# Pooled q and k of the first batch on GpSimd, and longer transfers in the plan, in a kernel whose order a planner writes

## The chip, the cores and the metric

The kernel runs on one core of one Trainium2 chip. The metric is the device time of one execution in microseconds (us); less is better. Three runs of the kernel before took 880.1, 879.05 and 879.85 us (median 879.85). The profile is of a further execution that took 879.63 us, of which 877.9 us are the span of its instructions.

## The reference

Attention comes first, then two dense layers. The inputs q, k and v are (4 batches, 8 heads, 576 positions, 64) in float32.

```
q_d, k_d, v_d = means of q, k, v over groups of 4 neighbouring positions   (144 positions)
out_up    = softmax(q_d k_d^T / 8) v_d, each row repeated 4 times
out_local = softmax over |i - j| < 4 of (q k^T / 8), times v
x = (out_up + out_local) as (2304 tokens, 512)
y   = (h * sigmoid(h), with h = x @ w_in) @ w_out                 # 512 -> 2048 -> 512
out = (h2 if h2 > 0 else exp(h2) - 1, h2 = y @ w_in2) @ w_out2    # the same sizes
```

## The kernel before

One stream of work is cut into jobs, and a planner inside the kernel's Python code decides, while the program is built, in which order each engine gets them. On the chip every engine then works its own list strictly in that order: an instruction at the head of a list that has to wait holds up all behind it.

**Jobs.** `Job(eng, dur, fn, preds, ...)` has an engine (P TensorE, V VectorE, A ScalarE, G GpSimd, S the transfer queue of SyncE), a reckoned duration, what it needs, buffers that it takes and gives back, and a due time. `alike(...)` makes a job that may run on either of two engines; the planner takes the one that would end earlier, with a bias from `PREFER`. `pick()` takes the job that can start first; between those that could start within 0.05 us it takes the one with the earlier due time, and on TensorE a job of the same kind as the last one is favoured by `STICK`. Transfers have a reckoned length: `D_ROWS` for q and k, `D_LOCAL` for windows of v, `D_V` for v to be pooled, `D_W` for a weight tile. `clock_of` says when each engine is first free in the plan.

**Fillers.** Up to the first full unit of the first dense layer, whenever the plan sees TensorE idle for longer than 0.1 us, `fill()` puts matmuls on zeros there (L370), one for each 0.22 us of the gap.

**Attention.** `attend(i, due)` makes the jobs for one pair of heads of one batch (16 pairs, 4 a batch). Rows of q and k are loaded, transposed on TensorE (L653), copied out of PSUM (L681, L686). `pool_qk` (L695) sums q and k over 4 neighbours, one VectorE reduction each. Local scores (L773, for batch 0 with the mask put in by matmul, L765) go through maximum, subtraction, exponential, sum, normalization (L784 on GpSimd) and transposition (L900). Pooled scores (L847) go through maximum (L861), exponential (L869), normalization (L886 on GpSimd), transposition (L921). L939 and L1005 multiply with v, L1022 joins both into x. `hED` is the tile of the pooled exponentials; batch 0 has two, `ring2` and a part of `yo`.

**Weights.** Tiles of 512 KB of the first dense layer land in three staging tiles (`ws`; one more is lent). `decode_jobs` turns the words of a tile into floats: two ScalarE passes (L426, L430) and three VectorE passes (L434, L437, L441); then ScalarE and GpSimd split each into a high and a low part (L1101, L1105). The next load into a staging tile waits for L441. Tiles are counted from 0; even ones are of w_in, odd ones of w_out.

**Dense layer 1** runs beside attention on blocks of 256 tokens: a unit is one product with a w_in tile (L1124, 12 matmuls, in chunks of 3 for the first two blocks), tanh on ScalarE, L1153 on VectorE, a split in two parts (L1155 on ScalarE, L1158 on GpSimd) and a product with a w_out tile (L1172, 12 matmuls). At most two PSUM banks hold units between L1124 and L1153. From some 200 us on, TensorE runs the remaining dense work (L1500, L1588, L1590) back to back.

Of the kernel before, what the change touches and what calls it, by code (L numbers as in the profile page):

```python
# [15 lines left out]
ALU = mybir.AluOpType  # L16
# [6 lines left out]
def attention_moe_moe2_kernel(ctx, tc, q, k, v, wi1, wo1, wi2, wo2, out):  # L23
# [29 lines left out]
    WIN = 64  # L53
    WARM = 9
    PREFER = {("G", "V"): 1.0, ("V", "G"): -1.0, ("A", "V"): 0.5, ("V", "A"): -0.5}
    PACKED, PE_POOLED, HALVED, CHUNKED, STICK, T_SECOND = 0, 1, 0, 4, 3, 40.0
    STICK_FROM = 0
    BACKLOG = 3.0
    D_ROWS, D_LOCAL, D_V, D_W, S_ROWS, S_LOCAL, X_AFTER = 1.6, 1.9, 1.5, 2.2, 1.1, 2.2, 1
    QUAD_FROM, MASK_PE = 0, 1  # L60
    FILL_TO, SAFE_R, SAFE_W = (0, 0), 0.0, 0.0
    LEND = 1
# [86 lines left out]
    cand, blocked = [], set()  # L149
    events = {}  # L150
    now = [0.0]
    clock_of = {"A": 0.0, "V": 4.0, "G": 4.0, "S": 0.0, "P": 5.0, "dma": 0.0, "port": 4.0}
    filling = [True]
    serial = [0]
    mode_of = [None]
# [252 lines left out]
    def decode_jobs(i, out, preds, takes=(), temp=None):  # L408
# [8 lines left out]
        if i < 2 * FP:  # L417
            held = [Hold(WS)]
            wst[i] = held[0]
            landed[i] = Job("S", 0.55, lambda: load_w(i), [], takes=held, dma=D_W, safe=SAFE_W)  # L420
        else:
            landed[i] = Job("S", 0.55, lambda: load_w(i), [decoded[i - WS_N]] if i >= 2 * FP + WS_N else [decoded[n] for n in range(2 * FP)], dma=D_W, safe=SAFE_W)

        def first():
            st = pairs_of(wst[i])
# [153 lines left out]
    def attend(i, due):  # L579
# [57 lines left out]
        def row_of(which, j, c):  # L637
            return (hq, hk)[which].tile[:, (j * NTB + c) * D:(j * NTB + c + 1) * D]

        copies = []  # L640
        prior = []
        for n_, cells in enumerate(([(0, c) for c in range(NTB - 1)], [(1, c) for c in range(NTB - 1)], [(0, NTB - 1), (1, NTB - 1)])):
            bank = Hold(banks, "a")
# [20 lines left out]
            for which in range(2):  # L664
                n = TB * sum(w == which for w, _ in cells)
                if n:
# [24 lines left out]


        def pool_qk():
            for which, src in enumerate(hqk.tile):
                nc.vector.reduce_sum(hqkD.tile[:, which * SD:(which + 1) * SD], src.rearrange("p (m r) -> p m r", r=FAC), axis=AX.X)  # L695

        red = Job("V", 1.48, pool_qk, copies, takes=[hqkD], uses=[hqk])
        vd = lambda: hvd.tile.rearrange("p (n d) -> p n d", n=4)
        pv = []
        if by_pe:  # L700
# [52 lines left out]
        for part, (s0, s1, halves_, outs) in enumerate(parts):  # L753
# [88 lines left out]
            def pooled_scores(halves_=halves_, bankd=bankd):  # L842
# [9 lines left out]
                        )  # L852

            psd = follow(Job(
                "P", 0.27 * len(halves_), pooled_scores, [red], lat=0.2, takes=bankd + ([hED, hsm] if start_ else []), uses=[hqkD], mode="d",
            ), "psd")
            exps = []
            for j, bank in enumerate(bankd):
# [753 lines left out]
    with tc.manual_schedule():  # L1612
# [29 lines left out]
        for i in range(len(pairs)):  # L1642
            b_, pr = pairs[i]
            if b_ == 0:
                attend(i, (11.0 + 4.0 * pr, T_SECOND + 4.0 * pr))
            else:
                lo_, hi_ = (at_[starts[b_ - 2], 0] if b_ > 1 else T_FIRST), at_[starts[b_ - 1], 0]
                if b_ > 1 and SOON:
                    attend(i, at_[starts[0], 0] - 6.0 + (i - 2 * NPAIR + 1) * SOON)
                    continue  # L1650
                attend(i, lo_ + (FRAC[pr] if b_ == 1 else (pr + 1) / NPAIR) * (hi_ - lo_) - 6.0)
        for n_ in range(NPAIR):
            late_v[n_].after([first_rows[min(n_ + 2, NPAIR - 1)]])
        for i in range(2 * FP):
            f, which = divmod(i, 2)
            pos = sequence.index((0, f))
            prepare(i, dues[pos] - 2.5 if which == 0 else dues[pos + LAG] - 2.5)
        for n in range(len(BLOCKS)):
            first_ = at_[n, 0] if n < len(BLOCKS) - 1 else at_[n - 1, 1]
            split_x(n, first_ - 1.5)  # L1660
# [94 lines left out]
```

## Time and profile before

| | before |
|---|---|
| median of 3 runs | 879.85 us |
| profiled execution | 879.63 us, span 877.9 us |
| TensorE busy | 865.9 us (99%) |
| VectorE busy | 668.7 us (76%) |
| ScalarE busy | 543.7 us (62%) |
| GpSimd busy | 251.5 us (29%) |
| transfers | 100.08 MB, mean 114 GB/s |

TensorE is the engine that the span belongs to, so a change can shorten the time only by what TensorE does not do usefully: idle stretches, fillers, stretches at the lower clock. Busy time in the first 60 us counts fillers as busy. The names in a row are the program's names of tiles, written before the arrow and read behind it.

### The profile page before, as it was taken

What the parts mean: (1) busy time and instruction counts of PE and PEld (TensorE: products, weight loads), DVE (VectorE), ACT (ScalarE), POOL (GpSimd) and SP (SyncE); (2) the same over time, 40 slices, a digit from 0 to 9 for tenths busy, and PEclk for the clock granted to TensorE, in tenths of its full rate; (3) what the DMA queues carried; (4) which work ended last, traced back from release to release, by engine and by line L of the source; (5) the groups of instructions that cost most, each with busy time, mean ns of one, the idle gap of its engine ahead of it and who ended that gap; (6) DMA issues with size and microseconds to landing.
All of it is one profiled execution on the core that took longest, in us unless ns stands there. A gap on an engine that the chain in (4) does not pass through costs nothing.

```text
span 877.9 us, 17291 instructions
## 1 busy us (share of the span) xinstructions
PE 865.9 (99%) x6632; PEld 809.7 (92%) x6640; DVE 668.7 (76%) x1255; ACT 543.7 (62%) x1228; POOL 251.5 (29%) x269
## 2 busy tenths in 40 slices
PE   8989999999999999999999999999999999999998
PEld 5779989999999999999999998898998998998986
DVE  8888777776968988979569879389489797493552
ACT  5787675564568568466377387385586684561750
POOL 4488786664103011301024213010141041010000
PEclk9989999999999999999999999999999999999999
DMA  9996377612123436253521340541420531310301
GB/s 170 205 219 173 81 202 180 169 49 97 56 90 121 132 103 221 77 173 125 178 92 52 109 156 1 166 123 60 132 72 37 174 126 37 111 70 37 108 0 72
DMA packets 105522, 100.08 MB, mean 114 GB/s; under 512 B 62240, under 2 KB 92448, under 8 KB 105312
## 3 DMA queue, kind: packets, MB, share of 16 engines
q1 hardware_dynamic: 103072, 98.39, 38.1%
q8 instruction: 52, 0.85, 0.4%
q10 hardware_dynamic: 2368, 0.59, 0.4%
q14 instruction: 30, 0.25, 0.1%
HBM read 75.37 MB, written 23.59 MB: 113 GB/s over the span
## 4 chain that ended last, share of the span: by engine, by line
PE 94%; DVE 2%; DMA 2%; issue 1%; ACT 0%; SPq 0%; POOL 0%; ACTq 0%; POOLq 0%; DVEq 0%
PE b L1500 33%; PE b L1590 22%; PE b L1588 15%; PE b L1172 8%; PE b L1124 7%; PE b L653 1%; PE b L1005 1%; PE b L921 1%; PE b L939 1%; PE b L900 1%; PE b L773 1%; PE b L847 1%; PE b L708 1%; DMA rows<-in_k_dram 1%; DMA ws<-in_moe_w_out_dram 1%; DMA rows<-in_q_dram 1%
## 5 line engine op out<-in xcount | busy, mean ns | idle before, releaser
L1590 PE MATMUL b<-w,grw 128*128 128x512 f32 x384 | 121.2, 389 | 0.0
L1590 PE MATMUL b<-w,ghk 128*128 128x512 f32 x288 | 99.1, 389 | 0.0
L1500 PE MATMUL b<-xhr,xaw 128*128 128x384 f32 x360 | 96.4, 335 | 0.0
L1588 PE MATMUL b<-grw,w 128*128 128x384 f32 x352 | 91.2, 334 | 0.0
L1590 PEld LDWEIGHTS b<-w,grw 128*128 128x128 f32 x384 | 72.1, 188 | 14.9
L1500 PE MATMUL b<-xhr,w 128*128 128x384 f32 x320 | 83.8, 335 | 0.0
L1124 PE MATMUL b<-xh,w 128*128 128x256 f32 x384 | 82.5, 293 | 1.2 <-DVE t L1153 0.7
L1172 PE MATMUL b<-gh,w 128*128 128x256 f32 x384 | 79.6, 288 | 0.0
L1590 PE MATMUL b<-w,glk 128*128 128x512 f32 x192 | 74.8, 389 | 0.0
L1588 PE MATMUL b<-ghk,w 128*128 128x384 f32 x248 | 71.6, 334 | 0.0
L1124 PEld LDWEIGHTS b<-xh,w 128*128 128x128 f32 x384 | 64.7, 194 | 3.0 <-DVE t L1153 0.9
L1500 PE MATMUL b<-xlr,xaw 128*128 128x384 f32 x200 | 66.9, 334 | 0.0
L1500 PEld LDWEIGHTS b<-xhr,xaw 128*128 128x128 f32 x360 | 65.5, 188 | 0.0
L1590 PEld LDWEIGHTS b<-w,ghk 128*128 128x128 f32 x288 | 54.1, 188 | 11.1
L1172 PEld LDWEIGHTS b<-gh,w 128*128 128x128 f32 x384 | 63.3, 191 | 0.7 <-ACT t L1152 0.2
L1588 PEld LDWEIGHTS b<-grw,w 128*128 128x128 f32 x352 | 63.7, 188 | 0.0
L1512 ACT COPY hg<-b 128x384 f32<-128x384 f32 x60 | 28.7, 480 | 52.5 <-PE b L1500 51.9
L1553 DVE SCALAR_TENSOR_TENSOR part<-b,part 128x384 f32<-128x384 f32 (+1 forms) x42 | 25.0, 609 | 44.8 <-PE b L1590 28.4
L1283 DVE TENSOR_TENSOR xlr<-tail,xhr 128x768 fp32r<-128x768 f32 x51 | 49.6, 973 | 11.5 <-ACT xhr L1280 11.2
L1500 PEld LDWEIGHTS b<-xhr,w 128*128 128x128 f32 x320 | 58.0, 188 | 0.2
L1588 PE MATMUL b<-glk,w 128*128 128x384 f32 x168 | 56.1, 334 | 0.0
L1280 ACT CAST xhr<-tail 128x768 fp32r<-128x768 f32 x60 | 50.0, 834 | 7.0 <-DVE tail L1361 4.3
(259 smaller groups left out, 2380.8 us busy)
## 6 DMA issues: line engine op xcount, KB each, us to landing
ws<-in_moe_w_in_dram SPq DMA_DIRECT2D x32, 512.0 KB
ws<-in_moe_w_out_dram SPq DMA_DIRECT2D x31, 512.0 KB
tail<-x SPq DMA_DIRECT2D x24, 384.0 KB
x<-part SPq DMA_DIRECT2D x6, 768.0 KB
out_dram<-part SPq DMA_DIRECT2D x18, 256.0 KB
vw<-in_v_dram SPq DMA_DIRECT2D x28, 144.0 KB
tail<-xd SPq DMA_DIRECT2D x10, 384.0 KB
natv<-in_v_dram SPq DMA_DIRECT2D x22, 144.0 KB
```

The source lines that it names most:

```text
L653: nc.tensor.transpose(bank.tile[:, n * TB:(n + 1) * TB], row(which, c)[:TB], ident[:TB, :TB])
L708: nc.tensor.matmul(bankv[j].tile[:HS, c * D:(c + 1) * D], pooler()[rows_, n, :], vw[rows_, w, :], start=n == 0, stop=n == len(POOLED_BY) - ...
L773: nc.tensor.matmul(held[j].tile[o:o + WIN, c:c + WIN], qT[j * D:(j + 1) * D, q0[w]:q0[w] + WIN], kT[j * D:(j + 1) * D, w0[w]:w0[w] + WIN], ...
L1124: nc.tensor.matmul(ph.tile[:, :NB0], w[a][:, c, :], x_slot(n, c, b_), start=start and m == 0, stop=stop and m == len(products) - 1,)
L1172: nc.tensor.matmul(y[d // 2].tile[:, o:o + NB0], w[m // 2][:, sl], gg(m % 2), start=f == 0 and m == 0 and d % 2 == 0, stop=fin and m == 2, ...
L1280: a = Job("A", ACT_[width], lambda: nc.scalar.copy(hi(), src), preds, gate)
L1283: other=("V", VEC_[width], lambda: nc.vector.tensor_tensor(lo(), src, hi().bitcast(F32), ALU.subtract)),
L1500: nc.tensor.matmul(acc_, a[:, cs], b[:, c, :], start=fresh and c == 0 and m == 0, stop=c == 1 and m == 2, skip_group_check=True,)
L1512: snap[after, j] = [Job("A", ACT_[NB], lambda dst=dst, acc_=acc_: nc.scalar.copy(dst, acc_), [], gate, due=soon)]
L1553: nc.vector.scalar_tensor_tensor(dst, src, sc, dst, op0=ALU.mult, op1=ALU.add)
L1588: nc.tensor.matmul(y[d][:, :NB], wm[:, sl], gm, start=first, stop=last_)
L1590: nc.tensor.matmul(y[d], gm[:, sl], wm, start=first, stop=last_)
```

## The change

Two edits of the program and several of the plan's numbers:

- For batch 0 q and k of a pair are pooled by two jobs, one each (`pool_one`, `pool_twice`), and each may run on GpSimd or on VectorE. On GpSimd it is two additions: elements 0 and 1 of each group of four to elements 2 and 3 (128x288), then the two half sums to one (128x144). The half sums stand in `hED`, so the pooling takes that tile earlier than the pooled scores did. Batches 1 to 3 are as before.
- The plan reckons transfers longer: v windows 2.3 instead of 1.9, v to be pooled 1.75 instead of 1.5, the first 16 weight tiles 2.5 instead of 2.2 (later ones stay at 2.2 as `D_LATE`); VectorE and GpSimd are first free at 7 instead of 4; `STICK` is 4 instead of 3; the splits of the first weights are due 1.5 us earlier, and the first half of batch 0's x 7 us later.

```diff
-    PACKED, PE_POOLED, HALVED, CHUNKED, STICK, T_SECOND = 0, 1, 0, 4, 3, 40.0
+    PACKED, PE_POOLED, HALVED, CHUNKED, STICK, T_SECOND = 0, 1, 0, 4, 4, 40.0
-    BACKLOG = 3.0
-    D_ROWS, D_LOCAL, D_V, D_W, S_ROWS, S_LOCAL, X_AFTER = 1.6, 1.9, 1.5, 2.2, 1.1, 2.2, 1
+    BACKLOG, D_LATE = 3.0, 2.2
+    POOL_G = 1
+    D_ROWS, D_LOCAL, D_V, D_W, S_ROWS, S_LOCAL, X_AFTER = 1.6, 2.3, 1.75, 2.5, 1.1, 2.2, 1
...
-    clock_of = {"A": 0.0, "V": 4.0, "G": 4.0, "S": 0.0, "P": 5.0, "dma": 0.0, "port": 4.0}
+    clock_of = {"A": 0.0, "V": 7.0, "G": 7.0, "S": 0.0, "P": 5.0, "dma": 0.0, "port": 7.0}
...
-        def pool_qk():
-            for which, src in enumerate(hqk.tile):
-                nc.vector.reduce_sum(hqkD.tile[:, which * SD:(which + 1) * SD], src.rearrange("p (m r) -> p m r", r=FAC), axis=AX.X)
-
-        red = Job("V", 1.48, pool_qk, copies, takes=[hqkD], uses=[hqk])
+        def pool_one(which):
+            nc.vector.reduce_sum(hqkD.tile[:, which * SD:(which + 1) * SD], hqk.tile[which].rearrange("p (m r) -> p m r", r=FAC), axis=AX.X)
+
+        def pool_twice(which):
+            x = hqk.tile[which].rearrange("p (m r) -> p m r", r=FAC)
+            z = hED.tile[:, which * 2 * SD:(which + 1) * 2 * SD].rearrange("p (m r) -> p m r", r=2)
+            nc.gpsimd.tensor_tensor(z, x[:, :, 0:2], x[:, :, 2:4], ALU.add)
+            nc.gpsimd.tensor_tensor(
+                hqkD.tile[:, which * SD:(which + 1) * SD].rearrange("p (m o) -> p m o", o=1), z[:, :, 0:1], z[:, :, 1:2], ALU.add
+            )
+
+        if b < POOL_G:
+            reds = []
+            for which in range(2):
+                reds.append(alike(
+                    1.25, lambda which=which: pool_twice(which), 0.74, lambda which=which: pool_one(which),
+                    [c for c, w_ in zip(copies, copied) if w_ == which], main="G", port=False, takes=[hqkD, hED] if which == 0 else [], uses=[hqk, hED],
+                ))
+            reds[1].after(reds[:1])
+            red = reds[1]
+        else:
+            red = Job("V", 1.48, lambda: [pool_one(which) for which in range(2)], copies, takes=[hqkD], uses=[hqk])
...
-                attend(i, (11.0 + 4.0 * pr, T_SECOND + 4.0 * pr))
+                attend(i, (18.0 + 4.0 * pr, T_SECOND + 4.0 * pr))
...
-            prepare(i, dues[pos] - 2.5 if which == 0 else dues[pos + LAG] - 2.5)
+            prepare(i, dues[pos] - 4.0 if which == 0 else dues[pos + LAG] - 4.0)
```

Because lines were added, lines of the changed kernel stand 1 (up to the pooling) or 19 (behind it) further down: L793 is L812 there, L861 is L880, L1124 is L1143, L1172 is L1191. Names of tiles carry the program's numbers; banks of PSUM are `b0` to `b7`.

First place: VectorE at the start, from the end of the constants on. `xb` holds the pooled q and k of batch 0, `small` the row statistics, `ring0` the local exponentials of the first pair. Before:

```order
L529 COPY natv_115<-natv_115 64x792
L695 TENSOR_REDUCE xb_88<-tail_89 128x144 x2
L793 TENSOR_REDUCE small_144<-b5_97 128x5
L793 TENSOR_REDUCE small_144<-b6_98 128x5
L798 TENSOR_TENSOR ring0_118<-b5_97,small_144 128x5x64
L798 TENSOR_TENSOR ring0_118<-b6_98,small_144 128x5x64
L861 TENSOR_REDUCE small_144<-b1_93 72x2
L861 TENSOR_REDUCE small_144<-b2_94 72x2
L695 TENSOR_REDUCE xb_88<-tail_89 128x144 x2
```

And with the change:

```order
L530 COPY natv_115<-natv_115 64x792
L812 TENSOR_REDUCE small_144<-b5_97 128x5
L812 TENSOR_REDUCE small_144<-b6_98 128x5
L817 TENSOR_TENSOR ring0_118<-b5_97,small_144 128x5x64
L817 TENSOR_TENSOR ring0_118<-b6_98,small_144 128x5x64
L880 TENSOR_REDUCE small_144<-b2_94 72x2
L880 TENSOR_REDUCE small_144<-b3_95 72x2
L847 TENSOR_REDUCE small_144<-ring0_118 128x10
L848 TENSOR_REDUCE small_144<-small_144 128x10
```

The reductions into `xb` are gone from here; in the whole of batch 0 one of eight stays on VectorE. The other seven stand on GpSimd, which has 14 additions more: four halves before its first normalization, three behind it.

Second place: the transfer queue (SyncE) behind batch 0's v, where weight tiles (`ws`, and `lent_137` for tile 3) and rows of batch 1 are issued (`lent_134`, `lent_136` and `nat0` are q and k, `lent_138` is v to be pooled, `vw0` are windows of v). Before:

```order
L400 DMA lent_137<-in_moe_w_out_dram 128x1024
L604 DMA lent_134<-in_q_dram 96x6x64 x2
L604 DMA lent_135<-in_k_dram 96x6x64 x2
L608 DMA lent_138<-in_v_dram 72x512 x2
L395 DMA ws_100<-in_moe_w_in_dram 128x4x256
L614 DMA vw0_116<-in_v_dram 64x9x64
L618 DMA vw0_116<-in_v_dram 64x64
L614 DMA vw0_116<-in_v_dram 64x9x64
L618 DMA vw0_116<-in_v_dram 64x64
L604 DMA lent_136<-in_q_dram 96x6x64 x2
L604 DMA nat0_113<-in_k_dram 96x6x64 x2
```

And with the change:

```order
L401 DMA lent_137<-in_moe_w_out_dram 128x1024
L396 DMA ws_100<-in_moe_w_in_dram 128x4x256
L605 DMA lent_134<-in_q_dram 96x6x64 x2
L605 DMA lent_135<-in_k_dram 96x6x64 x2
L609 DMA lent_138<-in_v_dram 72x512 x2
L615 DMA vw0_116<-in_v_dram 64x9x64
L619 DMA vw0_116<-in_v_dram 64x64
L615 DMA vw0_116<-in_v_dram 64x9x64
L619 DMA vw0_116<-in_v_dram 64x64
L401 DMA ws_101<-in_moe_w_out_dram 128x1024
L396 DMA ws_102<-in_moe_w_in_dram 128x4x256
```

Tile 4 stands ahead of batch 1's first rows, and tiles 5 and 6 ahead of its second pair; before, tile 5 was issued behind the rows of that pair.

Third place: TensorE around the first product with a w_out tile (`gh`, `gl` with `w1`). Before:

```order
L1124 MATMUL b4_96<-xl_747,w0_1041 128x256
L1124 MATMUL b4_96<-xh_746,w0_1041 128x256
L921 MATMUL b0_92<-ident_84,ring2_120 72x72 x4
L1124 MATMUL b4_96<-xh_746,w0_1041 128x256
L1124 MATMUL b4_96<-xl_747,w0_1041 128x256
L1124 MATMUL b4_96<-xh_746,w0_1041 128x256
L900 MATMUL b3_95<-ident_84,ring1_119 128x128 x3
L1124 MATMUL b4_96<-xh_919,w0_1041 128x256
L1124 MATMUL b4_96<-xl_920,w0_1041 128x256
L1124 MATMUL b4_96<-xh_919,w0_1041 128x256
L1172 MATMUL b0_92<-gh_145,w1_916 128x256
```

And with the change:

```order
L1143 MATMUL b2_94<-xh_624,w0_796 128x256
L1143 MATMUL b2_94<-xl_625,w0_796 128x256
L1143 MATMUL b2_94<-xh_624,w0_796 128x256 x2
L1143 MATMUL b2_94<-xl_625,w0_796 128x256
L1143 MATMUL b2_94<-xh_624,w0_796 128x256 x2
L1143 MATMUL b2_94<-xl_625,w0_796 128x256
L1143 MATMUL b2_94<-xh_624,w0_796 128x256
L1143 MATMUL b2_94<-xh_669,w0_796 128x256
L1143 MATMUL b2_94<-xl_670,w0_796 128x256
L1143 MATMUL b2_94<-xh_669,w0_796 128x256
L1191 MATMUL b1_93<-gh_145,w1_848 128x256
L1191 MATMUL b1_93<-gl_146,w1_848 128x256
```

Before, it stands behind products with three w_in tiles (`w0_728`, `w0_979`, `w0_1041`) and behind transposes for batch 1's third pair; now it stands right behind the product with the second w_in tile (`w0_796`). Ahead of it there are 62 fillers in the program instead of 48.

## Rows read from the trace of the kernel before

**Rows 1.** Busy time by stage: us, busy us (x instructions) per engine, granted clock, DMA share.

```profile
30.00:40.00 10.00, 8.30 (x191) 6.58 (x189) 8.71 (x23) 7.53 (x23) 6.58 (x8) 1.00 1.15 220
...
40.00:50.00 10.00, 9.70 (x180) 7.79 (x180) 9.92 (x20) 7.38 (x19) 5.48 (x8) 1.00 0.87 188
...
50.00:60.00 10.00, 7.87 (x78) 7.26 (x77) 7.67 (x18) 8.76 (x24) 8.74 (x10) 0.66 0.91 193
...
200.00:300.00 100.00, 100.00 (x754) 99.60 (x753) 80.12 (x154) 62.71 (x137) 21.87 (x19) 1.00 0.30 101
```

**Rows 2.** Timeline of TensorE: start us, us, what ran [idle before it <- releaser].

```profile
36.36 0.38 PE L370 MATMUL b<-t 128*128 128x512 bf16 x1 [1.65 <-issue]
...
47.21 0.47 PE L1124 MATMUL b<-xh,w 128*128 128x256 f32 x1
...
52.34 0.97 PE L653 MATMUL b<-ident,nat 96*128 96x96 f32 x5 [1.58 <-DMA nat<-in_q_dram]
...
55.29 0.58 PE L1124 MATMUL b<-xh,w 128*128 128x256 f32 x1 [0.54 <-DVE wf L441]
...
61.00 0.39 PE L1124 MATMUL b<-xh,w 128*128 128x256 f32 x1 [0.70 <-DVE t L1153]
...
63.41 0.28 PE L1172 MATMUL b<-gh,w 128*128 128x256 f32 x1
```

**Rows 3.** Busy time in two single microseconds, columns as in rows 1.

```profile
51.00:52.00 1.00, 0.00 (x0) 0.00 (x0) 0.00 (x0) 1.00 (x3) 0.46 (x2) 1.00 1.30 192
...
58.00:59.00 1.00, 1.00 (x6) 1.00 (x6) 0.94 (x3) 0.47 (x2) 0.73 (x2) 0.50 0.21 82
```

**Rows 4.** Timeline of VectorE: start us, us, what ran.

```profile
8.54 1.41 DVE L695 TENSOR_REDUCE xb<-tail 128x144 f32<-128x576 f32 x2
...
31.23 0.68 DVE L441 SCALAR_TENSOR_TENSOR wf<-ws,b 128x512 int32<-128x512 int32 x1
...
49.76 0.41 DVE L1153 SCALAR_TENSOR_TENSOR t<-t,b 128x256 f32<-128x256 f32 x1
...
52.26 0.70 DVE L434 TENSOR_SCALAR b<-b 128x512 f32<-128x512 f32 x1 [2.10 <-ACT b L426]
```

**Rows 5.** VectorE groups, 8 to 63 us: busy us, mean ns | idle before.

```profile
L437 DVE SCALAR_TENSOR_TENSOR b<-b,ws 128x512 int32<-128x512 int32 x6 | 4.1, 688 | 0.0
...
L695 DVE TENSOR_REDUCE xb<-tail 128x144 f32<-128x576 f32 x4 | 2.8, 743 | 0.0
...
L1022 DVE TENSOR_TENSOR xa<-b,ring 64x288 f32<-64x288 f32 x4 | 1.8, 454 | 0.1
...
L1153 DVE SCALAR_TENSOR_TENSOR t<-t,b 128x256 f32<-128x256 f32 x3 | 1.2, 405 | 0.0
...
L816 DVE TENSOR_REDUCE small<-ring 128x10 f32<-128x640 f32 x1 | 0.8, 809 | 0.0
```

**Rows 6.** GpSimd groups, 8 to 63 us.

```profile
L1105 POOL TENSOR_TENSOR w<-wf,w 128x512 fp32r<-128x512 f32 x5 | 6.3, 1277 | 4.6 <-ACT w L1101 4.6
...
L784 POOL TENSOR_TENSOR ring<-ring,small 128x640 f32<-128x640 f32 x5 | 6.3, 1261 | 10.4 <-DVE small L879 7.8 <-DVE small L830 2.6
...
L1070 POOL TENSOR_TENSOR xl<-xa,xh 128x256 fp32r<-128x256 f32 x8 | 5.7, 732 | 0.2 <-ACT xh L1066 0.2
...
L728 POOL TENSOR_TENSOR vd<-natv 72x128 f32<-72x128 f32 x2 | 0.9, 454 | 0.2
```

**Rows 7.** Timeline of TensorE and, last, the chain: pieces that price its work.

```profile
12.98 1.21 PE L653 MATMUL b<-ident,rows 96*128 96x96 f32 x12
...
33.62 0.45 PE L921 MATMUL b<-ident,ring 72*72 72x72 f32 x4
...
46.53 1.03 PE L370 MATMUL b<-t 128*128 128x512 bf16 x4
...
73.92 1.44 PE b L1172 x12
```

**Rows 8.** One ScalarE group, 8 to 63 us.

```profile
L1155 ACT CAST gh<-t 128x256 fp32r<-128x256 f32 x3 | 1.2, 410 | 0.3 <-DVE t L1153 0.3
```

More of the change, by code (lines that the diff above doesn't have):

```diff
@@ L421, in decode_jobs @@
         else:
-            landed[i] = Job("S", 0.55, lambda: load_w(i), [decoded[i - WS_N]] if i >= 2 * FP + WS_N else [decoded[n] for n in range(2 * FP)], dma=D_W, safe=SAFE_W)
+            landed[i] = Job("S", 0.55, lambda: load_w(i), [decoded[i - WS_N]] if i >= 2 * FP + WS_N else [decoded[n] for n in range(2 * FP)], dma=D_LATE, safe=SAFE_W)
         def first():
@@ L638, in row_of @@
             return (hq, hk)[which].tile[:, (j * NTB + c) * D:(j * NTB + c + 1) * D]
-        copies = []
+        copies, copied = [], []
         prior = []
@@ L688, in attend @@
                         )
+                    copied.append(which)
                     copies.append(alike(0.19 + 0.0008 * n, ops[0], 0.15 + 0.00106 * n, ops[1], [pj], uses=[bank]))
                     o += n
-        def pool_qk():
-            for which, src in enumerate(hqk.tile):
-                nc.vector.reduce_sum(hqkD.tile[:, which * SD:(which + 1) * SD], src.rearrange("p (m r) -> p m r", r=FAC), axis=AX.X)
-        red = Job("V", 1.48, pool_qk, copies, takes=[hqkD], uses=[hqk])
+        def pool_one(which):
[18 more added lines that the diff above has]
+            red = Job("V", 1.48, lambda: [pool_one(which) for which in range(2)], copies, takes=[hqkD], uses=[hqk])
         vd = lambda: hvd.tile.rearrange("p (n d) -> p n d", n=4)
@@ L854, in attend @@
             psd = follow(Job(
-                "P", 0.27 * len(halves_), pooled_scores, [red], lat=0.2, takes=bankd + ([hED, hsm] if start_ else []), uses=[hqkD], mode="d",
+                "P", 0.27 * len(halves_), pooled_scores, [red], lat=0.2, takes=bankd + ([hsm] + [hED] * (b >= POOL_G) if start_ else []), uses=[hqkD], mode="d",
             ), "psd")
```

## The prediction

> **What bounds the kernel now.** I read first the busy time by stage. From 200 us on TensorE is busy all the time [rows 1], and it has the same products to do with the change, so nothing is won or lost there. What the change can move lies in the first 65 us. There, between 40 and 50 us, VectorE is busy for 9.92 of 10 us and the transfers have a share of 0.87; between 50 and 60 us TensorE has 2.1 us idle and a mean granted clock of 0.66 [rows 1]. A clock that has only the levels 2.4 and 1.2 GHz and a mean of 0.66 was at the lower one for (1 - 0.66) x 2 x 10 = 6.8 us.
>
> Then the timeline of TensorE for who was waited for. It waits 1.65 us at 36.36 behind fillers, 1.58 us at 52.34 for rows of q that had not landed, 0.54 us at 55.29 for the third decode pass (it frees a bank) and 0.70 us at 61.00 for L1153 [rows 2]. The clock fell at the second of these: in the microsecond from 51 us TensorE did nothing at the full clock, and from 53 to 59 us it worked at 0.50 [rows 3]. The wait at 36.36 was as long and cost no clock: from 30 to 40 us it is 1.00 [rows 1]. The first unit of the first block has its last chunk at 47.21, and the first product with a w_out tile starts at 63.41 [rows 2]; from there TensorE is all but dense.
>
> The third view is VectorE's timeline: it is the engine that sets this stage. It starts on attention at 8.54, ends the first tile's decode at 31.9 and the first L1153 at 50.2, and then stands 2.1 us because ScalarE waits for a weight tile [rows 4].
>
> **What the change takes off VectorE and puts on GpSimd.** Seven of the eight reductions of batch 0 leave VectorE's list. One takes 743 ns alone and 0.70 us from start to start [rows 4, 5], so 7 x 0.70 = 4.9 us. GpSimd gets seven additions of 288 and seven of 144 elements. No row shows them, but others with two inputs take 0.73 us for 256, 1.28 us for 512 and 0.45 us for 128 elements [rows 6]; by the line through these, 0.80 and 0.50 us, 1.30 us for a half and 9.1 us in all. GpSimd is idle for 7.8 us in one piece ahead of its first L784 [rows 6], which covers four halves (5.2 us); the other three stand between normalizations that wait for VectorE anyway. What is not covered: the first pair's pooled scores need both halves, 2.6 us after the copies, where VectorE took 1.4 us but was then late for its own local scores. I put that at half a microsecond, made up by the end of the pair.
>
> The reading of four neighbours as pairs that stand 16 bytes apart is what no row shows. From below the price is the 1.30 us above; from above it is that of an addition that steps over every element that it passes (576 and 288 instead of 288 and 144): 1.42 + 0.80 = 2.2 us for a half. I take the lower end, since L784, which reads a broadcast operand, costs no more than the plain line [rows 6], and keep the upper for a rival. The Trainium skill (GPSIMD Engine Reference, section 7, Performance pitfalls) says that a read on GpSimd whose step is over 8 bytes costs half as much again for each element. By that rule, if it holds for a step between pairs, the larger addition would take an estimated 1.1 us and a half 1.6 us, 2.1 us more over seven halves; four of them lie in the idle stretch, the three others would delay the third and fourth pair by an estimated 0.3 to 0.6 us, and the sum below would be 878.6. No run here shows it.
>
> **What the moved jobs do on VectorE.** Up to the end of the first tile's decode the list holds 22.0 us of work before and 16.9 us now (each instruction by its step from start to start, the large ones in [rows 5]). From 8.5 us, with 1.9 us of waits as I find them following the order, the decode ends at 27.3 instead of 31.9. The transfer of tile 4, which needs this staging tile, then starts at once at 27.7, where before SyncE issued batch 1's first rows; these land one tile later (about 1.5 to 2 us), and nobody waits for them, since TensorE reaches them at 36.
>
> Then the gain is spent. Before the first L1153 the list held 39.7 us of work: 8.5 + 39.7 + 1.9 of waits is the 50.2 of the trace [rows 4]. Now it loses 4.9 us, but decodes three tiles more in front of it (4, 5 and 6: nine passes of 0.66 us from start to start, 5.9 us) and one L816 (0.8 us [rows 5]): 39.7 - 4.9 + 5.9 + 0.8 = 41.5 us. With waits of 2.6 us (I add 0.7 for GpSimd's normalization of the third pair), L1153 ends at 8.5 + 41.5 + 2.6 = 52.6 us, 2.4 us later than before, with 3 tiles more done.
>
> **What TensorE does with it.** The first product with a w_out tile needs, behind that L1153, L1155 (0.41 us [rows 8]) and the low part on GpSimd. GpSimd has an L784 in front of it, which waits for L816 and the split of tile 6: it runs 53.2 to 54.5, and the low part (0.73 us, as L1070 [rows 6]) ends at 55.2. TensorE has run out of work at 53.3 by my count, stands there for 2.0 us, and starts the product at 55.3, not at 63.41. From there: this product 1.44 [rows 7], local scores 0.75, a wait of 0.65 for the normalized exponentials, transposes 0.45, a wait of 0.4 for the next L1153 (58.9; one of two banks is free only then), 15 chunk products and two groups of transposes with 0.2 us of waits 2.5, the second product with a w_out tile 1.44: that ends at 63.3.
>
> Now the two lists side by side at 63.3 to 63.4. Both have done batch 0, 48 products with w_in tiles, and the same scores of batch 1. The changed kernel has done 24 products with w_out tiles more (2 x 1.44 = 2.88 us) and one group of L921 more (0.45); it has not done 17 transposes that the other has (17 x 1.21 / 12 = 1.7) [rows 7]. So it is 2.88 + 0.45 - 1.7 = 1.6 us ahead, and is dense from there as the other is. Further on, VectorE is some 3 us ahead with the decodes, which nothing asks for.
>
> 879.63 us of the profiled execution less 1.6 are 878.0. The median of the runs is 0.2 us above that execution, so this is 1.8 us below the median, just beyond the 0.2% (1.76 us) that a measurement of this kernel can tell from no change. I forecast 878.0.
>
> **STICK, due times and the rest.** The number of changes between kinds of products in the list is 89 now and 85 before: nothing. Due times and longer transfers act through the order alone, which is what I have followed.
>
> **Rivals.** (1) *No wait at the first product with a w_out tile.* If VectorE waits less than I let it, its L1153 is 2 us earlier, and TensorE gets another 2.0 us: 876.0. For it: the plan's transfers are now longer, as the waits at 52.34 and for tile 5 [rows 2, 4] say they should be. Against: VectorE was full in 40 to 50 us [rows 1], and its list has grown.
>
> (2) *The clock falls at that wait.* It is longer than the one at 52.34. If the lower level lasts 6.8 us as before [rows 1, 3], TensorE does 3.4 us of full-speed work in them. In my count it would do 6.8 less the waits of 0.65, 0.4 and 0.2, or 5.55. It loses 2.2 us: 878.0 + 2.2 = 880.2, no change. For it: 1.58 us sufficed once. Against: 1.65 us at 36.36 did not, nor does the stretch from 30 to 40 us, a sixth of it idle, show a fall [rows 1, 2].
>
> (3) *The fillers cost what they take: slower.* The list has 62 fillers, 14 more than before, 15 of them just ahead of the fourth pair's transposes, where I have the exponentials ready at 33.6 and the fillers' end at 34. One takes 1.03 / 4 = 0.26 us at most [rows 7], so 14 take 3.6 us. If what stands behind them is ready before they end, TensorE and not VectorE sets the first 48 us, all that VectorE saves is nothing, and the time is 879.8 + 3.6 = 883.4. It decides from the point where the normalization on GpSimd ends over 3 us ahead of the fillers. For it: the fillers stand in the list whether or not the wait that the plan sees is there on the chip. Against: before, TensorE stood behind its fillers for another 1.65 us [rows 2].
>
> (4) *GpSimd reads the pairs at the upper price.* Then a pair takes 4.4 us; the second pair's halves end at 16.8 instead of 13.9 us, and the first pair's L784, queued behind them on GpSimd, is 2.9 us late. VectorE, in order, waits for the exponentials behind it. 878.0 + 2.9 = 880.9.
>
> **Chances.** Forecast 0.38, with a range of its own of 876.5 to 879.8 (0.22 faster, 0.16 no change); rival 1 0.17 (faster); rival 2 0.20 (0.03, 0.10, 0.07 slower); rival 3 0.15 (0.13 slower, 0.02 no change); rival 4 0.10 (0.01, 0.05, 0.04). That makes 0.43 faster, 0.33 no change, 0.24 slower. The range reaches from 874.0, where rival 1 also loses the small waits that are left, to 882.5: about 0.05 lie below it and 0.13 above.
>
> **What would show it.** Right: seven reductions gone from VectorE before 20 us; additions of 288 at about 0.8 us; the first decode done near 27 us; the first L1191 at 55 to 56 us behind a wait of some 2 us on GpSimd's low part. Wrong: additions of 288 over 1.2 us; no idle time behind the 15 fillers; the first w_out product after 58 us; the mean granted clock of 50 to 60 us below 0.8; or other waits of over 1 us between 60 and 200 us, where I have counted none.

## Result, and the profile of the changed kernel

The changed kernel takes 885.91 us (median of 6 runs, 884.04 to 886.61) against 879.98 us (6 runs, 878.64 to 881.45): a ratio of 1.0053, 95% interval 1.003 to 1.0077. (Here and below the ratio is an estimate from all runs of both kernels, not the quotient of the two medians, which is 1.0067 here.) It is slower by about half a percent; 878.0 us had been forecast, with a range of 874.0 to 882.5. The profiled execution took 885.85 us, its span is 883.8.

First the busy time by stage (columns as in [rows 1]); the last line is a stretch of the paired stage.

```profile
50.00:60.00 10.00, 8.44 (x88) 7.22 (x90) 9.80 (x23) 8.19 (x23) 8.49 (x11) 0.89 1.16 214
200.00:300.00 100.00, 100.00 (x761) 98.99 (x760) 80.38 (x152) 60.69 (x136) 22.27 (x21) 1.00 0.28 96
360.00:370.00 10.00, 7.64 (x34) 7.08 (x33) 8.65 (x14) 3.84 (x8) 2.53 (x2) 0.83 0.00 0
```

The same stretch of the kernel before:

```profile
360.00:370.00 10.00, 10.00 (x59) 10.00 (x59) 9.15 (x13) 3.18 (x7) 4.30 (x3) 1.00 0.20 81
```

The stage to which the prediction gave its attention, 50 to 60 us, looks better than before (TensorE 8.44 us, clock 0.89). The stage that it set aside has a hole: 2.4 us of TensorE and a clock of 0.83. TensorE's timeline (columns as in [rows 2]) has the place, and the answers to [rows 2]:

```profile
33.68 2.76 PE L371 MATMUL b<-t 128*128 128x512 bf16 x12
36.28 0.49 PE L919 MATMUL b<-ident,ring 128*128 128x128 f32 x3
...
57.08 0.39 PE L1191 MATMUL b<-gl,w 128*128 128x256 f32 x1 [1.56 <-POOL gl L1177]
...
63.52 0.36 PE L1191 MATMUL b<-gh,w 128*128 128x256 f32 x1
...
360.83 0.34 PE L1607 MATMUL b<-glk,w 128*128 128x384 f32 x1
363.53 0.62 PE L1607 MATMUL b<-ghk,w 128*128 128x384 f32 x2 [2.36 <-DVE w L1302]
```

L1607 is a product of the paired stage's first pass, and `w` the last of its eight w_out tiles. (Behind the pooling a line's number is 19 higher than in the kernel before; L1302 was L1283.) The first product of the paired stage (L1519, before L1500) starts at 248.56 us, before at 247.41; the last one of the program at 879.50, before at 873.92. So 1.15 us are lost ahead of the paired stage and 4.43 us in it, from the first L1519 to the start of the last product. Another 0.3 us lie behind the last product, and 0.3 outside the span.

The chain of work that ended last (start, us, what) goes through the hole. Before, it ran on TensorE alone from some 195 us to the program's last products. Ahead of that it left TensorE for a few microseconds of VectorE and GpSimd at 122 and 188 us, and from 42.6 to 61.0 us for ScalarE, the transfer of a weight tile (5.70 us) and VectorE.

```profile
358.42 1.42 DVE raw L442
359.84 2.11 DVE ghk L1302
...
362.88 0.61 DVE w L1302
...
363.53 20.25 PE b L1607 x106
```

Two VectorE instructions stand in it with 1.42 and 2.11 us. VectorE's timeline, with four rows from the start, two of which answer to [rows 4]:

```profile
10.11 0.89 DVE L812 TENSOR_REDUCE small<-b 128x5 f32<-128x320 f32 x2 [1.60 <-PE b L792]
...
27.38 0.69 DVE L442 SCALAR_TENSOR_TENSOR wf<-ws,b 128x512 int32<-128x512 int32 x1
...
32.85 0.82 DVE L847 TENSOR_REDUCE small<-ring 128x10 f32<-128x640 f32 x1 [1.42 <-ACT ring L823]
...
53.75 0.41 DVE L1172 SCALAR_TENSOR_TENSOR t<-t,b 128x256 f32<-128x256 f32 x1
...
352.55 1.87 DVE L438 SCALAR_TENSOR_TENSOR raw<-raw,ws 128x512 int32<-128x512 int32 x1
...
357.74 0.68 DVE L1302 TENSOR_TENSOR w<-raw,w 128x512 fp32r<-128x512 f32 x1
358.34 1.50 DVE L442 SCALAR_TENSOR_TENSOR raw<-ws,raw 128x512 int32<-128x512 int32 x1
359.76 2.18 DVE L1302 TENSOR_TENSOR ghk<-hg,grw 128x384 fp32r<-128x384 f32 x1
361.87 1.01 DVE L1417 SCALAR_TENSOR_TENSOR hgx<-hgx,b 128x384 f32<-128x384 f32 x2
362.80 0.68 DVE L1302 TENSOR_TENSOR w<-raw,w 128x512 fp32r<-128x512 f32 x1
```

And GpSimd's: the pooling at the top, the first w_out product's low part (L1177) in the middle, the late place below.

```profile
8.81 0.67 POOL L701 TENSOR_TENSOR ring<-tail 128x288 f32<-128x288 f32 x1 [1.42 <-ACT tail L682]
9.56 0.42 POOL L702 TENSOR_TENSOR xb<-ring 128x144 f32<-128x144 f32 x1
...
52.53 2.60 POOL L1124 TENSOR_TENSOR w<-wf,w 128x512 fp32r<-128x512 f32 x2 [0.43 <-ACT w L1120]
55.09 1.25 POOL L803 TENSOR_TENSOR ring<-ring,small 128x640 f32<-128x640 f32 x1
56.30 0.72 POOL L1177 TENSOR_TENSOR gl<-t,gh 128x256 fp32r<-128x256 f32 x1
...
351.84 2.03 POOL L1301 TENSOR_TENSOR xlr<-tail,xhr 128x768 fp32r<-128x768 f32 x1
357.89 1.40 POOL L1301 TENSOR_TENSOR ghk<-hg,grw 128x384 fp32r<-128x384 f32 x1 [4.02 <-ACT grw L1299]
359.25 2.28 POOL L1301 TENSOR_TENSOR xlr<-tail,xhr 128x768 fp32r<-128x768 f32 x1
```

Lay the last three rows beside VectorE's. The subtractions end at 353.87, 359.29 and 361.53 us; VectorE's long instructions end at 354.42, 359.84 and 361.94, each 0.4 to 0.55 us later, which is about what such an instruction takes by itself. All three read two operands from SBUF. Read so, they waited for GpSimd's instruction; the run narrow, below, shows that they did. An L1527 at 352.08, beside the first subtraction but with an operand in PSUM, took 0.55 us. The Trainium skill (SBUF — State Buffer, "Who interferes with whom") has that rule: a VectorE instruction with two SBUF inputs contends with a GpSimd instruction that reads SBUF, the port that they share is an exclusive lock, and the order of issue decides who is held up. The trace agrees: the 0.55, 0.55 and 0.41 us that are left behind GpSimd's ends lie within 0.15 us of the 0.68, 0.68 and 0.55 us that such instructions take elsewhere.

In the kernel before, the same tile's passes stood 4.3 to 6.7 us earlier, the split ahead of three L1398 (now L1417):

```profile
354.00 0.68 DVE L441 SCALAR_TENSOR_TENSOR raw<-ws,raw 128x512 int32<-128x512 int32 x1
...
356.13 0.68 DVE L1283 TENSOR_TENSOR w<-raw,w 128x512 fp32r<-128x512 f32 x1
356.73 0.54 DVE L1398 SCALAR_TENSOR_TENSOR hg<-hg,b 128x384 f32<-128x384 f32 x1
```

The clock fell twice, at 58 us and behind the hole. Single microseconds (columns as in [rows 3], the granted clock third from the end):

```profile
60.00:61.00 1.00, 1.00 (x24) 0.88 (x16) 1.00 (x4) 0.41 (x1) 1.00 (x1) 0.50 1.13 173
...
365.00:366.00 1.00, 1.00 (x5) 1.00 (x4) 1.00 (x3) 0.96 (x3) 0.00 (x0) 0.52 0.00 0
366.00:367.00 1.00, 1.00 (x5) 1.00 (x5) 1.00 (x3) 0.91 (x2) 0.44 (x1) 0.50 0.00 0
367.00:368.00 1.00, 1.00 (x5) 1.00 (x4) 1.00 (x2) 0.00 (x0) 0.56 (x1) 0.50 0.00 0
368.00:369.00 1.00, 1.00 (x6) 1.00 (x5) 0.45 (x1) 0.00 (x0) 0.00 (x0) 0.77 0.00 0
```

Behind the hole that is 0.48 + 0.50 + 0.50 + 0.23 = 1.7 us of TensorE's work lost.

### The profile page after: what moved, and what is told of

Its sections match the earlier page's. It is cut to its first block, busy times and chain, and to the rows that moved or that the text cites. A ratio compares the mean times of both kernels' runs of the same rounds, so it can differ in the third digit from the quotient of the medians.

```text
span 883.8 us, 17329 instructions
## 1 busy us (share of the span) xinstructions
PE 872.3 (99%) x6654; PEld 812.4 (92%) x6654; DVE 671.9 (76%) x1249; ACT 542.9 (61%) x1227; POOL 258.6 (29%) x282
## 4 chain that ended last, share of the span: by engine, by line
PE 58%; DVE 1%; issue 0%
PE b L1519 26%; PE b L1609 22%; PE b L1607 10%; DVE ghk L1302 0%; DVE part L1572 0%; DVE raw L442 0%; DVE w L1302 0%; DVE b L1527 0%; DVE hgx L1417 0%; DVE raw L438 0%; DVE hg L1417 0%; DVE raw L435 0%
## 5 line engine op out<-in xcount | busy, mean ns | idle before, releaser
L1519 PE MATMUL b<-xhr,xaw 128*128 128x384 f32 x360 | 96.4, 335 | 0.0
L1607 PE MATMUL b<-grw,w 128*128 128x384 f32 x352 | 92.3, 337 | 0.0
L1519 PE MATMUL b<-xhr,w 128*128 128x384 f32 x320 | 83.8, 335 | 0.0
L1143 PE MATMUL b<-xh,w 128*128 128x256 f32 x384 | 81.1, 292 | 0.0
L1191 PE MATMUL b<-gh,w 128*128 128x256 f32 x384 | 80.4, 290 | 0.0
L1607 PE MATMUL b<-ghk,w 128*128 128x384 f32 x248 | 72.7, 338 | 2.4 <-DVE w L1302 2.4
L1519 PE MATMUL b<-xlr,xaw 128*128 128x384 f32 x200 | 66.9, 334 | 0.0
L1519 PEld LDWEIGHTS b<-xhr,xaw 128*128 128x128 f32 x360 | 65.5, 188 | 0.0
L1143 PEld LDWEIGHTS b<-xh,w 128*128 128x128 f32 x384 | 63.6, 191 | 1.4 <-issue 0.4
L1607 PEld LDWEIGHTS b<-grw,w 128*128 128x128 f32 x352 | 64.7, 190 | 0.0
L1191 PEld LDWEIGHTS b<-gh,w 128*128 128x128 f32 x384 | 63.6, 192 | 1.1 <-issue 0.6
L1302 DVE TENSOR_TENSOR xlr<-tail,xhr 128x768 fp32r<-128x768 f32 x51 | 50.1, 983 | 11.9 <-ACT xhr L1299 11.7
L1519 PEld LDWEIGHTS b<-xhr,w 128*128 128x128 f32 x320 | 58.0, 188 | 0.2
L1607 PE MATMUL b<-glk,w 128*128 128x384 f32 x168 | 56.3, 335 | 0.0
L1191 PE MATMUL b<-gl,w 128*128 128x256 f32 x192 | 54.6, 284 | 1.6 <-POOL gl L1177 1.6
```

What stands on the lines that cost most here:

```text
L1143: nc.tensor.matmul(ph.tile[:, :NB0], w[a][:, c, :], x_slot(n, c, b_), start=start and m == 0, stop=stop and m == len(products) - 1,)
L1191: nc.tensor.matmul(y[d // 2].tile[:, o:o + NB0], w[m // 2][:, sl], gg(m % 2), start=f == 0 and m == 0 and d % 2 == 0, stop=fin and m == 2, ...
L1302: other=("V", VEC_[width], lambda: nc.vector.tensor_tensor(lo(), src, hi().bitcast(F32), ALU.subtract)),
L1519: nc.tensor.matmul(acc_, a[:, cs], b[:, c, :], start=fresh and c == 0 and m == 0, stop=c == 1 and m == 2, skip_group_check=True,)
L1607: nc.tensor.matmul(y[d][:, :NB], wm[:, sl], gm, start=first, stop=last_)
```

## Experiments

In the table the paired stage's length is the start of the program's last product less that of its first L1519, in the run's profile. Medians are those of the runs; ratio and interval are against the kernel before on the same chip, whose medians there were 879.81 us (plan_only, pool_only, narrow, early8), 879.89 (hold, less, early8_hold, early8_hold_less) and 879.28 (before_late, before_hold, e6_less, e6_less35).

| kernel | median us | ratio (95%) | first L1519 | paired stage |
|---|---|---|---|---|
| before | 879.98 | | 247.41 | 626.51 |
| changed | 885.91 | 1.0053 (1.003 to 1.0077) | 248.56 | 630.94 |
| plan_only | 880.52 | 1.0005 (0.9982 to 1.0027) | 253.68 | 626.50 |
| pool_only | 885.57 | 1.006 (1.0038 to 1.0082) | 254.73 | 626.52 |
| narrow | 881.58 | 1.0008 (0.9989 to 1.0027) | 248.55 | 626.51 |
| early8 | 881.86 | 1.0014 (0.9998 to 1.003) | 248.15 | 627.73 |
| hold | 885.59 | 1.0061 (1.004 to 1.0081) | 248.34 | 630.87 |
| less | 884.2 | 1.0045 (1.0028 to 1.0062) | 247.84 | 630.64 |
| early8_hold | 882.18 | 1.002 (1.0002 to 1.0039) | 248.39 | 627.72 |
| early8_hold_less | 881.68 | 1.0016 (0.9995 to 1.0036) | 248.18 | 627.71 |
| before_late | 881.27 | 1.001 (0.9985 to 1.0034) | 246.35 | 626.62 |
| before_hold | 880.05 | 1.0001 (0.9983 to 1.0019) | 249.40 | 626.51 |
| e6_less | 880.79 | 0.9993 (0.9972 to 1.0015) | 248.34 | 626.51 |
| e6_less35 | 880.59 | 1.002 (0.9997 to 1.0044) | 251.09 | 626.50 |

The profiles of plan_only, pool_only, before_hold and e6_less35 are of executions 5.4, 1.8, 1.6 and 3.2 us over their medians, so their first L1519 stands later than in most of their runs; that of before_late is of one 2.5 us under its median. The kernel before itself ranges from 877.39 to 886.34 us over its 97 executions on these chips. One of early8_hold's 12 runs took 1729.54 us; its median is that of the other 11.

### Which part does it: plan_only, pool_only

```diff
-    POOL_G = 1                        # plan_only, on the changed kernel
+    POOL_G = 0
```

```diff
-    ... CHUNKED, STICK, T_SECOND = 0, 1, 0, 4, 4, 40.0     # pool_only, on the changed kernel
+    ... CHUNKED, STICK, T_SECOND = 0, 1, 0, 4, 3, 40.0
-    D_ROWS, D_LOCAL, D_V, D_W, ... = 1.6, 2.3, 1.75, 2.5, ...
+    D_ROWS, D_LOCAL, D_V, D_W, ... = 1.6, 1.9, 1.5, 2.2, ...
```

pool_only also takes back the engines' starting times (4.0) and the two due times (11.0 and 2.5).

> The changed kernel with POOL_G = 0: all numbers of the plan as changed, but all eight pooled halves as reductions on VectorE again. Main theory: the late wait of 2.36 us at 363.5 us comes from the place of the last w_out tile's decode in VectorE's row of the paired stage; in this kernel that row reads as in the kernel before (the tile's split ahead of the three L1417), so no wait over 0.5 us between 340 and 380 us, the first product of the paired stage (L1519) within 1.5 us of the kernel before's 247.4, and 879 to 882 us in all. Rival: any shift of the first stage by about a microsecond brings the late wait; then it stays at 1.5 to 2.5 us and the time is 884 to 886 us.

> The kernel before's numbers of the plan with batch 0's pooling on GpSimd or VectorE as changed. Main theory (order in the paired stage, made worse by GpSimd's subtractions beside it): VectorE's row there has one more subtraction (ghk) ahead of the last split and the L1417s behind it, so the late wait lies between none and the changed kernel's 2.36 us, about 0 to 1.2 us; first stage as the kernel before or up to 1 us shorter, since the changed kernel's first w_out tile and its clock fall at 55 us hang on the plan; 878 to 883 us. Rival (the pooling itself made the first stage slower): first L1519 at 248.5 us or later and 884 us or more.

The plan's numbers alone change nothing that can be measured, and their paired stage has no wait, as expected; where the first L1519 stands in a typical run of plan_only, its profile doesn't tell. The pooling alone costs 0.6%, outside the main theory's range and inside the rival's: its profile has no late wait, and all is lost in the first stage. There TensorE stands idle for 2.37 us in the middle of its 40 products with v, for nothing that the profile shows ("issue"), and the clock falls behind that:

```profile
34.93 0.73 PE L1024 MATMUL b<-ring,yo 64*64 64x60 f32 x33
38.03 0.34 PE L1024 MATMUL b<-ring,yo 64*64 64x57 f32 x7 [2.37 <-issue]
```

```profile
40.00:45.00 5.00, 5.00 (x35) 4.12 (x36) 2.77 (x5) 2.77 (x9) 2.21 (x4) 0.67 0.73 162
```

Why the first stage is so long without the plan's numbers stays open. With the change the same stage ends at 248.56 us, so there the pooling does better with the plan's numbers. Only together do the two make the late wait, which neither profile has alone: both have a paired stage of 626.5 us.

### What makes the late wait: narrow, early8, before_late

narrow, on the changed kernel, where `low_half` makes the subtractions that GpSimd made; it leaves most of three low halves unwritten:

```diff
+    def low_half(lo, x, hi):
+        made[0] += 1
+        if made[0] in (19, 20, 21):
+            lo, x, hi = [t[..., :8] for t in (lo, x, hi)]
+        nc.gpsimd.tensor_tensor(lo, x, hi, ALU.subtract)
```

early8, on the changed kernel (e6_less has 6.0); before_late is the kernel before with + 5.0:

```diff
-            job = two_jobs(..., gate(k), t0 + 28 * T_C + k * T_G)
+            job = two_jobs(..., gate(k), t0 + 28 * T_C + k * T_G - (8.0 if g == 1 else 0.0))
```

> The changed kernel, in which three GpSimd subtractions of the paired stage (those at 351.84, 357.89 and 359.25 us of the changed kernel's trace) work on 8 columns in the place of 384 of each half; it leaves the low halves of those three tiles unwritten beyond that. The order on every engine is the same. Main theory: VectorE's L438, L442 and L1302 beside them took 1.87, 1.50 and 2.18 us because they waited for GpSimd's instruction to end; without it they take 0.68, 0.68 and 0.55, the last split stands some 3.6 us earlier, the wait of 2.36 us at the last w_out tile and the lower clock behind it are gone, and the time falls by 3.5 to 4.5 us to 881.0 to 882.5. Rival (the order alone is late): the three VectorE instructions take 0.7 us at most and the wait at that tile is still over 1.5 us; time 884.5 to 886.

> The changed kernel, in which the plan's due time of the eight w_out splits of the first paired pass is 8 us earlier. The first stage's order is the same up to the paired stage; VectorE's row there has the last split w ahead of the three L1417 and of the ghk subtraction. Main theory: the split is done before 360 us, no wait over 0.5 us between 340 and 380 us, and the time is 881 to 882.5 us. Rival (what is taken from the end of the pass is late at its start: the split products, glk and L1527, now stand later): a wait of 1 us or more at another tile between 345 and 375 us and no gain, 884 to 886 us.

> The kernel before, whose only edit is that the eight w_out splits of the first paired pass are due 5 us later in the plan; the first stage is untouched. VectorE's row then reads as the changed kernel's: the last tile's split stands behind the ghk subtraction and three L1398. Theory (the late wait is made by that order, with GpSimd's subtractions beside it, and by nothing in the change itself): a wait of 1 to 2.5 us at the last w_out tile between 350 and 365 us, a granted clock of about 0.5 for some microseconds behind it, and 881 to 885 us. Rival (it takes the changed first stage too): no wait over 0.5 us there and 879.5 to 880.5 us.

narrow bears its main theory out. With the order of every engine as it was, VectorE's instructions are short and the split is done 3.6 us earlier (the helper moves the lines by 9):

```profile
357.14 0.68 DVE L442 SCALAR_TENSOR_TENSOR raw<-ws,raw 128x512 int32<-128x512 int32 x1
357.74 0.57 DVE L1311 TENSOR_TENSOR ghk<-hg,grw 128x384 fp32r<-128x384 f32 x1
...
359.17 0.68 DVE L1311 TENSOR_TENSOR w<-raw,w 128x512 fp32r<-128x512 f32 x1
```

No wait is left in the paired stage, the clock is at 1.00, and the stage is 4.43 us shorter: 2.36 of the wait, 1.7 of the lower clock behind it, and some 0.4 in the steps around the wait (the two products ahead of it take 0.53 us from start to start instead of 0.35, and the last one runs 0.34 us where the next start otherwise follows after 0.17). early8 gets the split out of the way instead and, as expected, has no wait over 0.5 us. It keeps 3.2 of these 4.4 us: an L442 at 352.13 takes 2.33 us beside GpSimd without harm, but two waits come up at the pass's start.

```profile
346.13 0.41 PE L1607 MATMUL b<-ghk,w 128*128 128x384 f32 x1 [0.47 <-DVE hg L1417]
347.11 0.44 PE L1607 MATMUL b<-ghk,w 128*128 128x384 f32 x1 [0.22 <-DVE hg L1417]
```

before_late leaves its theory open. In its profile, of a run of 878.75 us, the split stands behind a ghk subtraction and three L1398, as in the changed kernel, and no wait comes: the split takes 0.67 us, and it is GpSimd's subtraction that takes 3.81 us in the place of 2.0. VectorE, then GpSimd:

```profile
354.24 0.54 DVE L1283 TENSOR_TENSOR ghk<-hg,grw 128x384 fp32r<-128x384 f32 x1
...
355.18 0.67 DVE L441 SCALAR_TENSOR_TENSOR raw<-ws,raw 128x512 int32<-128x512 int32 x1
...
357.31 0.67 DVE L1283 TENSOR_TENSOR w<-raw,w 128x512 fp32r<-128x512 f32 x1
```

```profile
355.93 1.40 POOL L1282 TENSOR_TENSOR ghk<-hg,grw 128x384 fp32r<-128x384 f32 x1 [4.50 <-ACT grw L1280]
357.29 3.81 POOL L1282 TENSOR_TENSOR xlr<-tail,xhr 128x768 fp32r<-128x768 f32 x1
```

So in this execution a late place in VectorE's row is not enough. As the two traces read, it takes GpSimd's subtractions beside the last decode, at a moment when they hold VectorE up and not the other way round. But the order is not quite the changed kernel's: here the ghk subtraction stands ahead of the last decode pass, there behind it. And the median, 881.27 us, lies in the theory's range; five of the 12 runs took 881.95 to 885.19 us, and whether these had the wait no profile shows.

### What the clock costs at 57 us: hold, early8_hold, before_hold

hold, on the changed kernel (before_hold puts the same seven ahead of the transposes at 52.34 us in the kernel before):

```diff
         def second(ds):
             w = wt[f, 1]
+            if n == 0 and f == 0:
+                x = masks.rearrange("p a s w -> p (a s w)")
+                for _ in range(7):
+                    nc.tensor.matmul(y[0].tile, x[:, :P], x[:, :512], start=True, stop=True, skip_group_check=True)
```

> The changed kernel with seven filling products (128x512) on TensorE ahead of the first w_out product (L1191), into the same bank, which that product's start clears. Theory: they take 7 times 0.22 us in the 1.56 us in which TensorE waited there, the granted clock stays at 1.00 from 55 to 65 us (it was 0.50 from 59 to 61), the first product of the paired stage comes 1.5 to 1.8 us earlier than 248.6, and the time is 884.0 to 884.5, with the late wait at 363 us as in the changed kernel. Rival: VectorE and GpSimd set the pace from 50 to 65 us, so that TensorE at the full clock only waits later for the same splits; then the clock stays up and the first L1519 gains less than 0.5 us.

> The changed kernel with both: w_out splits of the first paired pass due 8 us earlier, and the seven filling products ahead of the first L1191. If late wait and lower clock at 57 us are the two losses and are independent, 885.9 less 4.0 and less 1.7 is 880.2; 879.7 to 880.7 us. If the paired stage's gain hung on where the first stage ended, the wait at the last w_out tile would come back at 1 us or more, 883 us or more.

> The kernel before with seven filling products (128x512) ahead of the transposes that wait 1.58 us at 52.34 us, in their own bank. Theory of the prediction (the lower clock from 51 to 58 us costs TensorE up to 2 or 3 us): the clock stays at 1.00 and the time falls by 1.5 to 3 us, to 877 to 878.4. Rival, as in the changed kernel with such products (VectorE and GpSimd set the pace from 50 to 65 us): the clock stays up, TensorE waits as much longer behind, and the time stays within 0.7 us of the kernel before.

In hold the rival holds: 885.59 us for 885.91, with the clock at 1.00 and TensorE waiting elsewhere:

```profile
56.97 0.39 PE L1195 MATMUL b<-gl,w 128*128 128x256 f32 x1 [0.26 <-POOL gl L1177]
...
59.89 0.55 PE L919 MATMUL b<-ident,ring 128*128 128x128 f32 x3 [0.60 <-POOL ring L803]
```

```profile
55.00:60.00 5.00, 4.15 (x61) 2.87 (x61) 4.83 (x13) 3.85 (x13) 4.50 (x7) 1.00 1.09 220
```

VectorE is busy 4.83 and GpSimd 4.50 of 5 us: they set the pace, and a TensorE at half clock follows them as well. narrow shows it without any filling product. It has the wait of 1.56 us too, its clock did not fall, and its first L1519 stands at 248.55, the changed kernel's at 248.56. early8_hold misses both of its expectations for the same reason: the late wait stays away, and the filling products win nothing (882.18 us for early8's 881.86).

before_hold takes the time of the kernel before (880.05 us for 879.28, a ratio of 1.0001), but it doesn't test the rival: the wait at 52.34 us fell from 1.58 to 0.31, other waits grew, and the clock fell all the same, 7 us later. So what the fall costs in the kernel before stays open:

```profile
54.68 0.38 PE L1128 MATMUL b<-xh,w 128*128 128x256 f32 x1 [1.09 <-DVE wf L441]
```

```profile
60.00:65.00 5.00, 4.58 (x22) 4.58 (x23) 4.01 (x9) 3.50 (x9) 5.00 (x5) 0.50 1.21 249
```

### Fillers, and the best version: less, early8_hold_less, e6_less, e6_less35

```diff
-        filler(min(int((gap - 0.1) / 0.22), 40))
+        filler(min(int(0.6 * (gap - 0.1) / 0.22), 40))     # e6_less35: 0.35
```

> The changed kernel with each group of filling products (L371) cut to 0.6 of its number, 36 in the place of 62; the order of all else is as it was. Theory of the fillers (TensorE was busy 10.00 of 10 us from 30 to 50, fillers ended 0.75 us after what they waited for): the first decode and the first w_out product come 0.5 to 1.5 us earlier, first L1519 at 247.0 to 248.1 us, 884.4 to 885.4 in all. Rival: with fewer fillers the clock falls in the gaps between 20 and 50 us; then products there take twice as long, first L1519 stands at 249 us or later, 886.5 us or more.

> The same with the filling products of the first stage cut to 0.6 of their number too. Theory of the fillers: 0.5 to 1.5 us under the run without that cut, 878.7 to 880.2 us. Rival (the clock falls between 20 and 50 us): 1 us or more above it.

> The changed kernel with the w_out splits of the first paired pass due 6 us earlier (they were 8 in an earlier run, which moved 0.7 us of waits to 346 us) and 0.6 of the filling products. If the two gains add up: 885.9 less 4.3 and less 0.7 to 1.2 is 880.4 to 880.9, with no wait over 0.3 us between 340 and 380 us. If the order of the splits is late again at another tile: 882 or more.

> The same with 0.35 of the filling products. If TensorE's fillers still stand in the way of the scores between 20 and 50 us, 0.3 to 0.7 us less than with 0.6 of them; if the granted clock falls in the gaps, 1 to 5 us more, with a clock under 0.9 in some stretch from 20 to 50 us.

With 36 fillers in the place of 62, TensorE waits where it had been filling, and is earlier:

```profile
33.29 1.69 PE L371 MATMUL b<-t 128*128 128x512 bf16 x7
35.58 0.52 PE L919 MATMUL b<-ident,ring 128*128 128x128 f32 x3 [0.60 <-POOL ring L803]
```

L919 starts at 35.58, not 36.28, the second w_out product at 62.80, not 63.52, and the first L1519 0.72 us earlier. In these two executions that is the fillers' price; the median, 884.2 us, lies 0.2 under its expected range. The other pairs show less of it: early8_hold_less is 0.5 us under early8_hold in the median and 0.2 us ahead at the first L1519, and misses its 878.7 to 880.2; e6_less, at 248.34, is not ahead of early8's 248.15. In both TensorE stands idle at 46 us, for 0.80 and 0.57 us, for nothing that the profile shows; in less that is 0.25 us.

With 0.35 of the fillers the median is 0.2 us lower than with 0.6, less than expected; three of its 12 runs take 882.77 to 888.53 us, and the profile of one of these shows a clock of 0.87 from 40 to 50 us. e6_less is the steadiest version with the change: no wait in the paired stage, 880.13 to 881.36 us with a median of 880.79, as expected. By the interval (0.9972 to 1.0015) it is not to be told from the kernel before, whose median on that chip is 1.5 us lower. No version is shown to be faster than the kernel before.

## Why the prediction was wrong, step by step

**The step that failed** is the first one: from 200 us on TensorE has the same products to do and is always busy, "so nothing is won or lost there". It rested on a row that shows TensorE busy [rows 1]. Such a row does not show how much room the engines that feed it have. VectorE's last split was done 2.36 us late in a row that the plan had written anew down to the end of the program; of 7.85 us between forecast and profiled execution, 4.43 lie there, and narrow gives back all of them. The sum follows the new order to 63 us and no further. So do the signs: of its five signs of being wrong only one came (no idle time behind the 15 fillers), and none of them looks beyond 200 us.

**The pooling on GpSimd** was dearer in the forecast than it is: 0.80 and 0.50 us taken, 0.67 and 0.42 measured, 1.1 us a half. Rival 4 is out. So is the estimate of 1.1 us for the larger addition, made from the Trainium skill (GPSIMD Engine Reference, section 7, Performance pitfalls) for the case that its rule holds for a step between pairs. The Trainium skill speaks there of the inner step, and within a pair that is 4 bytes, so the 0.67 us contradict the estimate and not the rule.

**The walk along the order** found the right places and was 1 to 2 us early. First decode done at 27.3, measured 28.1; first L1172 done at 52.6, measured 54.2; wait at the first w_out product 2.0 on GpSimd's low part, measured 1.56 on the same; its low part's product at 55.3, measured 57.1. In the forecast the L803 ahead of it ran from 53.2 to 54.5; in fact two L1124 held GpSimd until 55.1. VectorE's row up to the first L1172 shows the term that was too small: its work is 41 us, as reckoned, but its waits (those over 0.1 us) add up to 4.5 us instead of 2.6. The largest are 1.60 at 10.11 us for TensorE's local scores, where two reductions had filled the time before, and 1.42 at 32.85 for ScalarE's exponentials. less shows 0.7 us of the lateness to be fillers in its execution: rival 3's mechanism, at a fifth of its price.

**The sum at 63.3 us.** The terms written out add up to 62.9, or 63.1 with the 0.2 us of waits counted apart, not to 63.3. The second w_out product ends at 65.0 (63.52 and twelve products), 1.65 us behind the 63.3. The lists side by side gave 1.6 us of lead; added up over TensorE's timeline from there to the first paired product, without waits, they are 183.14 us before and 182.56 now, a lead of 0.6. The 17 transposes more cost about 1.0 us, not 1.7, which helped; but the four L921 less gave nothing, not 0.45, and the w_in products took about 1.0 us and the transposes of L900 0.4 us more between other neighbours. 1.65 + 1.0 + 0.1 of waits are the 2.75 us between the 1.6 forecast as won and the 1.15 lost.

**Rivals.** Rival 2's event came (0.50 from 58 to 61 us, half as long as taken), its price did not: it counted TensorE's lost work where TensorE was not the bound. Rival 3's 883.4 is near the time by accident. The argument against it misread a row: the 1.65 us at 36.36 stand ahead of one more filler and not behind the last, and TensorE waits there for nothing that the profile shows. No rival had the late wait. Other waits between 60 and 200 us stay at 0.52 or less, as forecast.

## What to carry to other kernels

Where a planner writes the order, a change of its early numbers rewrites all that follows: read the new order against the old wherever another engine feeds a dense one, and price how late its last delivery may be, not how busy the dense engine is. A VectorE instruction with two SBUF operands beside a GpSimd one cost up to nearly GpSimd's whole length here (0.55 us became 2.18), so such subtractions don't belong beside a chain without slack. A lower clock, like any slow engine, cost time here only where that engine was the bound.

## What had not been expected of the hardware

- VectorE and GpSimd, each reading two operands from SBUF: 0.55 us on VectorE became 2.18 beside a GpSimd subtraction of 2.28; turned round (before_late), one of 2.0 on GpSimd became 3.81.
- A wait of 1.56 us brought the clock to 1.2 GHz in one execution (changed kernel) and not in another with the same first stage (narrow). Seven filling products did not keep it up in before_hold, where it was 0.50 from 60 to 65 us.
- After the late wait the clock was low for some 3.4 us, which cost 1.7 us there, where TensorE was the bound; 3.4 us of it at 58 us cost nothing that shows (the paired stage begins at 248.56 us, in narrow without the fall at 248.55).
- GpSimd's addition of pairs 16 bytes apart: 0.67 us for 288 elements, less than 0.73 for a subtraction of 256 in a row [rows 6].
